# Six k loads of the first steps on ScalarE's queue, and the expert weights by half pairs, in an attention, mixture-of-experts and GELU kernel

## The chip, the cores and the metric

The kernel runs on one core of one Trainium2 chip. The metric is the device time of one execution in microseconds (us); lower is better.

## What is computed

Three layers follow each other. The first is a decayed linear attention (4 batches, 8 heads, 768 positions, 64 channels), the second a soft mixture of 8 experts with 4 slots each, the third a feed-forward layer with a sigmoid-GELU.

```python
for b in range(nb):                       # attention, block by block
    intra = einsum('bhic,bhjc->bhij', qb, kb) * Dmask
    intra = einsum('bhij,bhjd->bhid', intra, vb)
    inter = einsum('bhid,bhde->bhie', qb * lam_pow, kv_state)
    out[:, :, sl] = intra + inter
    kv_state = lam_block * kv_state + einsum('bhsd,bhse->bhde', kb * rev_pow, vb)
...
logits = x @ phi                          # x: 3072 x 512, phi: 512 x 32
slot_input = softmax(logits, 0).T @ x
h = maximum(slot_input[e] @ w1[e], 0.0)   # w1[e]: 512 x 1024
slot_out[e] = h @ w2[e]                   # w2[e]: 1024 x 512
x = softmax(logits, 1) @ slot_out
...
h = x @ w_in                              # w_in: 512 x 2048
return (h * (1.0 / (1.0 + exp(-1.702 * h)))) @ w_out
```

## The kernel before, in words

**Stages.** The attention comes first (to about 147 us of the profiled execution), then the experts (about 152 to 186 us), then the feed-forward layer, which is matmul after matmul to the end.

**Attention.** It has 32 steps (`NSTEP`), one for each pair of heads, half sequence (384 positions) and batch. The loop over `i` runs from -2 to 31 and is a hand-written pipeline under a manual schedule: in one round it does the scores of step i+1 (`do_SC`), the transposes of q and k of step i+2 (`do_T`, line 271 for q, 273 for k), the copy of q of step i+3 into another layout on ScalarE (`do_q`, line 262), the states (`do_ST`), the decayed k of step i+2 on ScalarE (`do_kd`, line 297) and the output of step i (`do_XS`, `do_XA`). Every fourth round does more, the tail of a finished group of four steps: logits, softmax pieces and slot sums.

**Loads.** `load_step` fetches q by one transfer (192 KB, line 126), and k and v by two transfers of 96 KB each, one per head (line 131). Their rooms are rings: three for q and three for k (pool `loads`), four for v. A load into a used room waits for the last reader of the step that had it. Before the change every one of these transfers is issued by SyncE (SP), whose queue takes them in the order of the program.

**Expert weights.** They are 32 pairs of 1 MB; `load_pair` issues one transfer per pair (line 170), or two of 512 KB for two of the pairs (line 168). Sixteen pairs have rooms of their own during the attention (`slots`), and `load_pairs(i)` decides how many of them are issued by round i. The other 16 wait for rooms that are freed at the attention's end (`slotb`, `slotc`) or by experts that are done. After them SP's queue has the first loads of the last layer's weights.

**Semaphores.** A transfer takes one of eight completion semaphores by turns, over both issuing engines together. An issue waits until the transfer that had its semaphore before has landed.

**Start.** ScalarE issues the load of `lam_b` (line 493), then loads its activation table and copies q of step 0. TensorE does eight warm-up matmuls meanwhile (line 501).

Of the kernel before, what the change touches and what calls it, by code (L numbers as in the profile page):

```python
# [17 lines left out]
def attention_moe_gelu_kernel(  # L18
# [14 lines left out]
    PE, ACT, DVE, POOL, SP = nc.tensor, nc.scalar, nc.vector, nc.gpsimd, nc.sync  # L33

    B, H, S, D = q.shape
    P = 128
    NHP = H // 2
    HS = 384
# [11 lines left out]
    NSTEP = NG * NHP  # L50
    NE = 1
    NPC = 16
# [58 lines left out]
    q_r, q_t, k_t, v_t = {}, {}, {}, {}  # L111

    def step_of(s):
        g, hp = divmod(s, NHP)
        b, hf = divmod(g, NHF)
        return b, hf, hp, g

    def load_step(s, what="qkv"):
        if s >= NSTEP:
            return  # L120
        b, hf, hp, g = step_of(s)
        t0 = hf * HS
        if "q" in what:

            q_r[s] = loads.tile([P, 2, R * D], F32, tag="qr", name="qr")
            SP.dma_start(out=q_r[s], in_=q[b, 2 * hp:2 * hp + 2, t0:t0 + HS, :].rearrange("h (p c) d -> p h (c d)", p=P))
        for src, nm, ts, bufs, pool in ((k, "k", k_t, 3, loads), (v, "v", v_t, 4, attn)):
            if nm in what:
                t = pool.tile([P, R, 2, D], F32, tag=nm, name=nm, bufs=bufs)
                for h in range(2):  # L130
                    SP.dma_start(out=t[:, :, h, :],  # L131
                                 in_=src[b, 2 * hp + h, t0:t0 + HS, :].rearrange("(c p) d -> p c d", p=P))
                ts[s] = t

# [4 lines left out]
    PC = 1024  # L139
    w_pc = {}  # L140
    worder = [("w1", 0)] + [we for e in range(1, E) for we in (("w1", e), ("w2", e - 1))] + [("w2", E - 1)]
    wlist = [(kind, e, j) for kind, e in worder for j in range(0, KD, 2)]
    nxt_w = [0]

    def pair_room(n):
        m = n % (NPC + NPC_B + NPC_C + NPC_D)
        if m == NPC + NPC_B + NPC_C:
            return [tailp.tile([P, PC], F32, tag="xn", name="w") for _ in range(2)]
        if m < NPC:
            return slots.tile([P, 2 * PC], F32, tag="w", name="w")  # L150
        return (slotb if m < NPC + NPC_B else slotc).tile([P, 2 * PC], F32, tag=f"w{m}", name="w", bufs=1)

    def load_pair(t=None):

        n = nxt_w[0]
        if n >= len(wlist):
            return
        nxt_w[0] += 1
        kind, e, j = wlist[n]
        if t is None:  # L160
            t = pair_room(n)
        src = w1[e, j * P:(j + 2) * P, :] if kind == "w1" else w2[e]
        src = src.rearrange("(p k) f -> p (k f)", p=P)
        o = 0 if kind == "w1" else j * PC
        parts = t if isinstance(t, list) else [t[:, :PC], t[:, PC:]]
        if isinstance(t, list) or n == len(wlist) - 1:
            for i in range(2):
                SP.dma_start(out=parts[i], in_=src[:, o + i * PC:o + (i + 1) * PC])
        else:
            SP.dma_start(out=t, in_=src[:, o:o + 2 * PC])  # L170
        w_pc[kind, e, j], w_pc[kind, e, j + 1] = parts
# [68 lines left out]
    def do_early(c):  # L240
        o = EARLY[c][-1]
        convert_abs(("early", c), o)
        by_turns(conversion(("early", c), o, POOL))
# [14 lines left out]
    def do_q(s):  # L258

        if s < NSTEP:  # L260
            q_t[s] = early.tile([P, R, 2, D], F32, tag="q", name="q", bufs=1)
            ACT.activation(out=q_t[s].rearrange("p c h d -> p h c d"),
                           in_=q_r[s].rearrange("p h (c d) -> p h c d", c=R), func=AF.Copy)
# [227 lines left out]
    with tc.manual_schedule():  # L491
# [7 lines left out]
        def warm_up(n):  # L499
            for _ in range(n):  # L500
                PE.matmul(bwarm, warm[:, :P], warm, start=True, stop=True)

        warm_up(8)
        for s, what in ((0, "qk"), (1, "qk"), (0, "v")):
            load_step(s, what)
        do_q(0)
        for h in range(2):
            r = slice(h * D, (h + 1) * D)
# [2 lines left out]
        def make_dec(h):  # L511

            DVE.tensor_tensor_scan(out=dec[:, h], data0=lam_b[:, h:h + 1].to_broadcast([P, P]), data1=ident,
                                   initial=0.0, op0=ALU.mult, op1=ALU.add)
# [4 lines left out]
        n = 1  # L519
        while n < P:  # L520
            DVE.tensor_tensor(out=qtab[:, :, n:2 * n], in0=qtab[:, :, 0:n],
                              in1=qtab[:, :, n - 1:n].to_broadcast([P, NHP, n]), op=ALU.mult)
            n *= 2
        load_step(1, "v")
        load_step(2, "k")
        load_step(2, "q")
        load_step(3, "q")
        for t in S_a + S_3:
            POOL.memset(t, 0.0)
# [2 lines left out]
        def make_isum():  # L532
            for j in range(G):
                for i in range(G):
                    POOL.tensor_copy(out=isum4[i * NS:(i + 1) * NS, j, :],
                                     in_=ident[i * NS:(i + 1) * NS, i * NS:(i + 1) * NS])

        def load_pairs(i):
            n = min(NPC, max(0, i + 1) * NPC // (NSTEP - 1), NPC - 1 if i < NSTEP - 5 else NPC)
            while nxt_w[0] < n:  # L540
                load_pair()

        for i in range(-2, NSTEP):
            g, ph = divmod(i, NHP)
            if i > -2:
                load_step(i + 5, "q")
            if i == 1:
                make_isum()

            if 0 <= i + 1 < NSTEP:  # L550
                do_SC(i + 1)
            if 0 < i + 2 < NHP:

                for h in range(2):
                    make_dec(2 * (i + 2) + h)

            if 0 <= i + 2 < NSTEP:
                do_T(i + 2)
                if i == -2:
                    warm_up(1)  # L560
            if i == NSTEP - 1:
                do_XS(i)
            if 0 <= i - 1 < NSTEP:
                do_XT(i - 1)
            if 0 <= i + 3 < NSTEP:
                do_q(i + 3)
            if ph == 1 and 0 <= g - 1 < NG:
                tail_L(g - 1)
            if ph == 2 and 0 <= g - 1 < NG:
                tail_max(g - 1)  # L570
            if ph == 3 and 0 <= g - 1 < NG:
                tail_exp(g - 1)
            if i == NSTEP - 1:
                tail_logits_first(NG - 1)
            if 0 <= i < NSTEP - 1:
                do_XS(i)

            if 0 <= i + 1 < NSTEP:
                do_ST(i + 1)
            if 0 <= i + 2 < NSTEP:  # L580
                do_kd(i + 2)
            if 0 <= i < NSTEP:
                do_XA(i)

            if ph == 0 and 0 <= g - 1 < NG:
                tail_logits(g - 1)
            if ph == 0 and 0 <= g - 2 < NG:
                tail_z(g - 2, "tk")
                tail_slot(g - 2)
                tail_acc(g - 2)  # L590
            if i == NSTEP - 4:
                load_pairs(i + 1)

            load_pairs(i)

            load_step(i + 5, "k")
            if i >= -1:
                load_step(i + 4, "v")
            c, turn = divmod(i - 2, EVERY)
            if turn == 1 and 0 <= c + 1 < len(EARLY):  # L600
                load_early(c + 1)
            if 0 <= i + 2 < NSTEP:
                do_qd(i + 2)
            if i == -2:
                load_step(2, "v")
                SP.dma_start(out=phi_sb, in_=phi.rearrange("(k p) s -> p k s", p=P))
            if turn == 0 and 0 <= c - 1 < len(EARLY):
                do_early(c - 1)
            if ph == 3 and 0 <= g - 1 < NG and i < NSTEP - 1:
                tail_row(g - 1)  # L610
            if ph == 0 and 0 <= g - 2 < NG:
                tail_row_exp(g - 2)
            if i == NSTEP - 3:
                while nxt_w[0] < NPC:
                    load_pair()
                loads_cm.__exit__(None, None, None)
                slotb_cm = tc.tile_pool(name="slotb", bufs=NPC_B, side="right", reuse_waits="tile")
                slotb = slotb_cm.__enter__()

                rooms = [pair_room(NPC + j) for j in range(NPC_B)]  # L620
                for t in rooms[::-1]:
                    load_pair(t)
            if i == NSTEP - 1:
                attn_cm.__exit__(None, None, None)
                early_cm.__exit__(None, None, None)
                slotc_cm = tc.tile_pool(name="slotc", bufs=NPC_C, side="left", reuse_waits="tile")
                slotc = slotc_cm.__enter__()
                rooms = [pair_room(NPC + NPC_B + j) for j in range(NPC_C)]
                for t in rooms:
                    load_pair(t)  # L630
# [219 lines left out]
        for f in range(2, NF):  # L850
            j = first_of[f] - 2 if f < HF else LATE_OUT.get(f, first_of[f] - 1)
# [68 lines left out]
        for kk in range(KD):  # L920
            src = bso[kk][:, None, :NS].to_broadcast([P, G, NS])
# [450 lines left out]
```

## Time and profile before

| | before |
|---|---|
| median of three runs | 476.57 us (475.67 to 476.94) |
| the profiled execution's own time | 477.57 us |
| its span, first to last instruction | 475.8 us |
| TensorE busy | 464.5 us, 98% of the span |
| DVE, ScalarE, GpSimd busy | 373.8, 302.7, 79.3 us |
| granted TensorE clock, mean | 0.999 of full speed |
| moved by DMA | 81.52 MB |

Busy time is what an engine spends in its own instructions; SP has none of those, its time is that of the transfers that it issues ("SPq", and "ACTq" for those that ScalarE issues). A transfer's landing is counted from its issue. "DMA share" is the mean busy share of the core's 16 DMA engines in a stretch.

### The profile page before, as it was taken

The numbers are of one execution on the slowest core, as the hardware profiler recorded it, in microseconds if no ns is written. First come the engines' busy times: TensorE is split into PE (matmuls) and PEld (weight loads), VectorE is DVE, ScalarE is ACT, GpSimd is POOL, SyncE is SP. The second block draws the span as 40 slices with busy tenths as digits, with TensorE's granted clock in tenths as the row PEclk, the third lists the DMA queues.
The fourth block names the chain that finished last, engine by engine and source line by source line (L and its number), as shares of the span: only waits on it lengthen the run. The fifth ranks groups of instructions, "written<-read, shape, count | busy, mean of one in ns | idle before, by whom it ended". The sixth has DMA issues, their size and how long they took to land.

```text
span 475.8 us, 10619 instructions
## 1 busy us (share of the span) xinstructions
PE 464.5 (98%) x3991; PEld 387.6 (81%) x3991; DVE 373.8 (79%) x901; ACT 302.7 (64%) x606; POOL 79.3 (17%) x129
## 2 busy tenths in 40 slices
PE   7999999999999998999999999999999999999996
PEld 4877877887876444787888778888899999999996
DVE  5866988988974344897787689998779989888985
ACT  5877678677754146866865867576665565565561
POOL 3624444444221010000000000000001111011104
PEclk9999999999999999999999999999999999999999
DMA  7899999999999997465643532100323331233034
GB/s 186 230 275 294 293 275 280 269 280 300 257 322 412 416 421 288 123 216 190 222 125 101 219 133 90 44 0 1 115 65 45 46 45 17 30 45 45 2 46 90
DMA packets 77476, 81.52 MB, mean 171 GB/s; under 512 B 54256, under 2 KB 62960, under 8 KB 73584
## 3 DMA queue, kind: packets, MB, share of 16 engines
q1 hardware_dynamic: 74832, 76.50, 51.2%
q0 software_dynamic: 2304, 4.20, 6.6%
q8 instruction: 32, 0.52, 0.5%
q14 instruction: 20, 0.16, 0.1%
q10 hardware_dynamic: 288, 0.14, 0.1%
HBM read 69.80 MB, written 11.01 MB: 170 GB/s over the span
## 4 chain that ended last, share of the span: by engine, by line
PE 80%; DMA 9%; DVE 6%; SPq 1%; issue 1%; ACT 1%; POOLq 0%; ACTq 0%; DVEq 0%
PE bo L1027 26%; PE bp L1195 25%; DMA w<-in_moe_w_dram 6%; PE bs L309 4%; PE bx L356 3%; PE bx L348 3%; PE bsh L1150 2%; PE bhh L980 2%; PE bq L271 2%; PE bst L322 2%; DMA qr<-in_q_dram 2%; PE bt L367 2%; PE bk L273 2%; DMA k<-in_k_dram 1%; SPq L131 1%; PE bp L449 1%
## 5 line engine op out<-in xcount | busy, mean ns | idle before, releaser
L1027 PE MATMUL bo<-wlo,GHI 128*128 128x512 f32 x192 | 75.3, 395 | 0.1
L1164 ACT ACTIVATE GHI<-G_all 128x896 fp32r<-128x896 f32 x48 | 45.8, 955 | 46.4 <-DVE G_all L1157 46.1
L1027 PE MATMUL bo<-whi,GLO 128*128 128x512 f32 x192 | 75.1, 394 | 0.0
L1027 PE MATMUL bo<-whi,GHI 128*128 128x512 f32 x192 | 74.8, 393 | 0.1
L1157 DVE TENSOR_TENSOR G_all<-G_all 128x128 f32<-128x128 f32 x192 | 47.3, 288 | 18.6 <-ACT G_all L1153 16.0
L1225 POOL DMA_DIRECT2D out_dram<-f x16 | 14.2, 1047 | 278.8 <-DVE G_all L1157 264.1
L1195 PE MATMUL bp<-tc,GHI 128*128 128x256 f32 x288 | 55.9, 282 | 0.0
L1169 DVE TENSOR_TENSOR GLO<-G_all,GHI 128x896 fp32r<-128x896 f32 x48 | 52.0, 1084 | 0.0
L988 ACT ACTIVATE G_all<-bhh 128x384 f32<-128x384 f32 x64 | 28.2, 489 | 34.5 <-PE bhh L980 34.4
L1195 PE MATMUL bp<-whi,GHI 128*128 128x256 f32 x192 | 49.5, 281 | 0.0
L1195 PE MATMUL bp<-wlo,GHI 128*128 128x256 f32 x192 | 49.2, 282 | 0.0
L1195 PE MATMUL bp<-whi,GLO 128*128 128x256 f32 x168 | 47.5, 283 | 0.0
L1195 PEld LDWEIGHTS bp<-tc,GHI 128*128 128x128 f32 x288 | 44.4, 190 | 0.0
L1027 PEld LDWEIGHTS bo<-wlo,GHI 128*128 128x128 f32 x192 | 36.0, 188 | 9.6 <-issue 2.5
L1027 PEld LDWEIGHTS bo<-whi,GLO 128*128 128x128 f32 x192 | 36.0, 188 | 7.8 <-DVE GLO L994 0.3
L1027 PEld LDWEIGHTS bo<-whi,GHI 128*128 128x128 f32 x192 | 36.1, 188 | 7.6 <-DVE W2s L934 0.5
L1195 PE MATMUL bp<-tc,GLO 128*128 128x256 f32 x144 | 40.4, 280 | 0.0
L290 POOL TENSOR_TENSOR qdT<-qT,qtab 128x384 f32<-128x384 f32 x32 | 32.4, 1014 | 40.7 <-PE bx L348 18.4
L994 DVE TENSOR_TENSOR GLO<-G_all,GHI 128x768 fp32r<-128x768 f32 x32 | 30.5, 954 | 10.5 <-ACT GHI L991 10.2
L1195 PEld LDWEIGHTS bp<-wlo,GHI 128*128 128x128 f32 x192 | 34.7, 189 | 0.0
L1195 PEld LDWEIGHTS bp<-whi,GHI 128*128 128x128 f32 x192 | 34.6, 189 | 0.0
L309 PEld LDWEIGHTS bs<-qT,kT 64*128 64x128 f32 x384 | 25.0, 187 | 11.8 <-DVE zsum L469 4.2
(234 smaller groups left out, 1036.7 us busy)
## 6 DMA issues: line engine op xcount, KB each, us to landing
w<-in_moe_w_dram SPq DMA_DIRECT2D x30, 1024.0 KB, 7.1
f<-in_moe_w_out_dram SPq DMA_DIRECT2D x15, 512.0 KB, 3.4
qr<-in_q_dram SPq DMA_DIRECT2D x32, 192.0 KB, 4.3
k<-in_k_dram SPq DMA_DIRECT2D x64, 96.0 KB, 5.5
v<-in_v_dram SPq DMA_DIRECT2D x64, 96.0 KB, 4.5
f<-in_moe_w_in_dram SPq DMA_DIRECT2D x12, 512.0 KB, 3.8
out_dram<-o SPq DMA_DIRECT2D x24, 256.0 KB, 2.6
out_dram<-f POOLq DMA_DIRECT2D x16, 256.0 KB, 4.8
```

The lines of the kernel that those rows point to most:

```text
L290: POOL.tensor_tensor(out=qdT[s], in0=qT[s].rearrange("m (c i) -> m c i", c=R), in1=qtab[:, hp, None, :].to_broadcast([P, R, P]), op=ALU.mult)
L309: PE.matmul(bs[h][:, cs], kT[s][hs, cs], qT[s][hs, cs], start=True, stop=True)
L348: PE.matmul(bx[:, c * P:(c + 1) * P], state(s, first + c), qdT[s][:, c, :], start=(c == chunks[0]), stop=False)
L356: PE.matmul(bx[h * D:(h + 1) * D, c * P:(c + 1) * P], v_t[s][:, c, h, :], AT[s, h][:, c, :], start=False, stop=(c == R - 1))
L988: ACT.activation(out=g[j][:, u * HS:(u + 1) * HS], in_=bh[j][u][:, :HS], func=AF.Gelu_apprx_sigmoid)
L994: DVE.tensor_tensor(out=glo[j][:, o], in0=g[j][:, o], in1=ghi[j][:, o].bitcast(F32), op=ALU.subtract)
L1027: PE.matmul(ob[t], a[j][:, t * P:(t + 1) * P], w[f], start=(begin and i == 0), stop=(end and i == 2))
L1157: DVE.tensor_tensor(out=o, in0=x, in1=y, op=op)
L1164: ACT.activation(out=sh[j], in_=gs(j)[:, P:], func=AF.Copy)
L1169: DVE.tensor_tensor(out=sl[j], in0=gs(j)[:, P:], in1=sh[j].bitcast(F32), op=ALU.subtract)
L1195: PE.matmul(bank_of(gi, i)[1], x, w, start=begin, stop=end)
L1225: POOL.dma_start(out=rows_of(gi, k), in_=cells[:, C11 + 2 * k:C11 + 2 * k + 2], accum_op=ALU.add)
```

## The change

Two things change. First, the k transfers of steps 0, 1 and 2 (six of them) are issued by ScalarE rather than by SP, ahead of ScalarE's first copy; q of step 2 moves ahead of v of step 1 on SP. Second, the 16 weight pairs that are loaded during the attention are each fetched by two transfers of 512 KB (`load_half`), and `load_pairs` counts halves: one per round from round -1 on, where before it was one whole pair about every second round from round 1 on.

```diff
-    def load_step(s, what="qkv"):
+    def load_step(s, what="qkv", eng=SP):
...
-            SP.dma_start(out=q_r[s], in_=q[b, 2 * hp:2 * hp + 2, t0:t0 + HS, :].rearrange("h (p c) d -> p h (c d)", p=P))
+            eng.dma_start(out=q_r[s], in_=q[b, 2 * hp:2 * hp + 2, t0:t0 + HS, :].rearrange("h (p c) d -> p h (c d)", p=P))
...
-                    SP.dma_start(out=t[:, :, h, :],
+                    eng.dma_start(out=t[:, :, h, :],
...
+    half_done = []
+
+    def load_half():
+
+        n = nxt_w[0]
+        kind, e, j = wlist[n]
+        src = w1[e, j * P:(j + 2) * P, :] if kind == "w1" else w2[e]
+        src = src.rearrange("(p k) f -> p (k f)", p=P)
+        o = 0 if kind == "w1" else j * PC
+        if not half_done:
+            half_done.append(pair_room(n))
+            SP.dma_start(out=half_done[0][:, :PC], in_=src[:, o:o + PC])
+            return
+        t = half_done.pop()
+        nxt_w[0] += 1
+        SP.dma_start(out=t[:, PC:], in_=src[:, o + PC:o + 2 * PC])
+        w_pc[kind, e, j], w_pc[kind, e, j + 1] = t[:, :PC], t[:, PC:]
...
-        for s, what in ((0, "qk"), (1, "qk"), (0, "v")):
-            load_step(s, what)
+        for s, what, eng in ((0, "q", SP), (0, "k", ACT), (1, "q", SP), (1, "k", ACT), (0, "v", SP), (2, "q", SP),
+                             (2, "k", ACT)):
+            load_step(s, what, eng)
...
         load_step(1, "v")
-        load_step(2, "k")
-        load_step(2, "q")
         load_step(3, "q")
...
-            n = min(NPC, max(0, i + 1) * NPC // (NSTEP - 1), NPC - 1 if i < NSTEP - 5 else NPC)
-            while nxt_w[0] < n:
-                load_pair()
+            n = min(2 * NPC, max(0, (i + 3) * 2 * NPC // (NSTEP + 1)), 2 * NPC - 2 if i < NSTEP - 5 else 2 * NPC)
+            while 2 * nxt_w[0] + len(half_done) < n:
+                load_half()
...
                 while nxt_w[0] < NPC:
-                    load_pair()
+                    load_half()
```

ScalarE's first instructions before, with the semaphores that they wait for (`lam_b` holds the decays, `qr` the loaded q, `bq` and `bk` the transposes of q and k):

```order
L493 DMA lam_b<-in_lam_dram 128x8
L262 ACT_TABLE_LOAD
L262 ACTIVATE q<-qr 128x2x3x64 [waits DMAHW1_49]
L281 ACTIVATE qT<-bq 128x3x128 [waits PE_49]
L284 ACTIVATE kT<-bk 128x384 [waits PE_49]
```

The same place of the changed kernel:

```order
L511 DMA lam_b<-in_lam_dram 128x8
L131 DMA k<-in_k_dram 128x3x64 x3
L131 DMA k<-in_k_dram 128x3x64 [waits DMAHW0_49]
L131 DMA k<-in_k_dram 128x3x64 [waits DMAHW2_49]
L131 DMA k<-in_k_dram 128x3x64 [waits DMAHW4_49]
L280 ACT_TABLE_LOAD
L280 ACTIVATE q<-qr 128x2x3x64 [waits DMAHW1_49]
```

Six issues now stand ahead of the table load, and the last three wait for semaphores: 0 is that of `lam_b`, 2 and 4 are those of the two k transfers of step 0.

SP's queue at the end of the attention before, from round 26 to the pairs whose rooms are freed (a `w` of 128x2048 is a whole pair, one of 128x1024 a half):

```order
L131 DMA k<-in_k_dram 128x3x64 x2
L131 DMA v<-in_v_dram 128x3x64 x2
L170 DMA w<-in_moe_w_dram 128x2048
L131 DMA v<-in_v_dram 128x3x64 x2
L170 DMA w<-in_moe_w_dram 128x2048 x7
```

The same place of the changed kernel:

```order
L131 DMA k<-in_k_dram 128x3x64 x2
L131 DMA v<-in_v_dram 128x3x64 x2
L164 DMA w<-in_moe_w_dram 128x1024
L131 DMA v<-in_v_dram 128x3x64 x2
L168 DMA w<-in_moe_w_dram 128x1024
L164 DMA w<-in_moe_w_dram 128x1024
L168 DMA w<-in_moe_w_dram 128x1024
L188 DMA w<-in_moe_w_dram 128x2048 x5
```

Behind the last v there were seven pairs; now there are three halves and five pairs, 512 KB less.

## Rows read from the trace of the kernel before

**Rows 1.** The page's first part: span, then TensorE's busy time, share and instructions.
```profile
span 475.8 us, 10619 instructions
...
PE 464.5 (98%) x3991; PEld 387.6 (81%) x3991; DVE 373.8 (79%) x901; ACT 302.7 (64%) x606; POOL 79.3 (17%) x129
```

**Rows 2.** Chain that ended last, 148 to 190 us: start, us, what.
```profile
154.88 12.23 DMA w<-in_moe_w_dram
...
167.12 17.53 DMA w<-in_moe_w_dram
...
184.70 1.05 PE bacc L789 x4
```

**Rows 3.** Timeline of PE, expert stage: start, us, instruction [idle before, releaser].
```profile
173.30 1.92 PE L789 MATMUL bacc<-w,hz 128*32 128x512 f32 x16
...
180.62 0.45 PE L736 MATMUL bc<-identr,cs 128*128 128x128 f32 x3
182.23 2.24 PE L789 MATMUL bacc<-w,hz 128*32 128x512 f32 x12 [1.16 <-DMA w<-in_moe_w_dram]
```

**Rows 4.** Busy time by stretch: length, engines, granted clock, DMA share, GB/s.
```profile
core 0: us, PE busy (x) PEld busy (x) DVE busy (x) ACT busy (x) POOL busy (x), PEclk, DMA share, GB/s
0.00:4.00 4.00, 3.23 (x8) 1.02 (x8) 0.10 (x1) 1.28 (x1) 1.91 (x15) 1.00 0.42 96
...
8.00:12.00 4.00, 3.08 (x44) 2.55 (x44) 3.81 (x13) 2.95 (x7) 1.34 (x3) 1.00 0.93 226
12.00:24.00 12.00, 12.00 (x173) 10.59 (x171) 9.60 (x31) 9.75 (x25) 7.67 (x20) 1.00 0.87 232
24.00:48.00 24.00, 22.53 (x285) 18.07 (x283) 16.71 (x48) 17.52 (x44) 8.73 (x11) 1.00 1.04 287
...
142.00:146.00 4.00, 3.98 (x43) 2.78 (x37) 1.39 (x6) 2.13 (x6) 0.35 (x1) 1.00 0.92 350
...
160.00:168.00 8.00, 8.00 (x116) 3.54 (x112) 2.67 (x6) 0.95 (x2) 0.94 (x3) 1.00 1.01 418
...
176.00:185.00 9.00, 7.17 (x68) 2.27 (x70) 3.29 (x11) 6.93 (x14) 0.00 (x0) 1.00 1.01 411
```

**Rows 5.** Timeline of the start, all engines.
```profile
0.73 0.45 ACTq L493 DMA_DIRECT2D lam_b<-in_lam_dram  x1
...
0.74 0.43 SPq L126 DMA_DIRECT2D qr<-in_q_dram  x1
...
1.21 1.28 ACT L262 ACT_TABLE_LOAD   x1 [1.21 <-PEq L1356]
1.23 0.99 SPq L131 DMA_DIRECT2D k<-in_k_dram  x2
...
3.90 0.34 DVE L509 COPY lamb<-lam_b 64x4 f32<-64x4 f32 x2 [3.90 <-DMA lam_b<-in_lam_dram]
4.13 0.52 ACT L262 ACTIVATE q<-qr 128x384 f32<-128x384 f32 x1 [1.64 <-DMA qr<-in_q_dram]
...
4.80 0.52 PE L271 MATMUL bq<-ident,q 128*128 128x128 f32 x3 [0.48 <-ACT q L262]
...
8.40 0.49 ACT L284 ACTIVATE kT<-bk 128x384 f32<-128x384 f32 x1
...
9.93 0.52 ACT L262 ACTIVATE q<-qr 128x384 f32<-128x384 f32 x1 [1.04 <-DMA qr<-in_q_dram]
```

**Rows 6.** DMA issues of 1.2 to 1.7 us: count, KB, us to landing.
```profile
k<-in_k_dram SPq DMA_DIRECT2D x1, 96.0 KB, 3.1
```

**Rows 7.** SP's waits, whole span: waiter, releaser, us in total, times, longest.
```profile
SPq L131 <- DMA w<-in_moe_w_dram: 3.6, 12, 0.7
```

**Rows 8.** Timeline of PE at the transposes of k, step 10.
```profile
43.20 0.52 PE L273 MATMUL bk<-ident,k 128*128 128x128 f32 x3 [1.05 <-DMA k<-in_k_dram]
```

**Rows 9.** Timeline of SP's queue at the attention's end.
```profile
131.21 0.48 SPq L170 DMA_DIRECT2D w<-in_moe_w_dram  x1
...
134.98 11.52 SPq L170 DMA_DIRECT2D w<-in_moe_w_dram  x7
```

## The prediction

> **What bounds the kernel now.** I read the page first: TensorE is busy 464.5 of 475.8 us [rows 1], so there are only 11.3 us in which it does nothing, and a change to transfers can give back no more than the part of these that waits for data. The chain that ended last shows where that is. In the expert stage it leaves TensorE: 12.23 and 17.53 us of it are landings of expert weights, the last at 184.66 us, and only then do the last four matmuls run [rows 2]. The stretches agree: at 160 to 168 us the DMA engines are fully busy at 418 GB/s [rows 4], and at 176 to 185 us TensorE is busy 7.17 of 9 us. So the experts end when the last weight lands, and everything later follows at TensorE's pace: a microsecond earlier or later there is a microsecond of the kernel.
>
> How much could be had there? Behind the last transposes at 180.62 + 0.45 us stand 16 matmuls, which without waits take about the 1.92 us of the 16 from 173.30 us on [rows 3]; they would end near 183.0 us, but end at 184.70 + 1.05 = 185.75 us [rows 2]. **Earlier weights are worth at most some 2.8 us**, as long as the attention doesn't end later.
>
> In the attention TensorE is the pace: 12.00 of 12 us at 12 to 24, 22.53 of 24 at 24 to 48 [rows 4]. The 1.47 us missing in the latter are nearly all one late k: 1.05 us at the transposes of step 10 [rows 8]. The DMA engines are at a share of about 1 from 24 us on, but are not full before: 0.93 at 8 to 12 us and 0.87 at 12 to 24, which leaves 4 x 0.07 + 12 x 0.13 = 1.84 us of them unused. At the start, step 2's q lets ScalarE wait 1.04 us [rows 5]: SP needs about 0.5 us for each issue (0.99 for two) and reaches that q late.
>
> **Edit 1: the weights by halves, sooner.** The order shows that behind the last v of the attention three halves and five pairs follow, where seven pairs did: 512 KB are ahead of that point. From there the engines are full until the last weight, so all that is gone from the backlog is gone from its end: 524,288 bytes at 418 GB/s [rows 4] are **1.25 us** earlier. It is a gain only if the DMA engines had room earlier (the 1.84 us say that they had) and if rooms don't hold the next pairs up. The pairs behind wait for rooms: SP's seven issues from 134.98 stretch over 11.52 us [rows 9], and at 142 to 146 us the rate falls to 350 GB/s [rows 4], (418 - 350) / 418 x 4 = 0.65 us below the full rate. If halves refill that dip the gain is 1.25 + 0.65 = 1.9 us; if the dip deepens by all that is saved, 0. I take 1.25, since the backlog behind the dip is long (the chain's landings last 12 to 18 us) and a pair's work is 2.5 us. The 16 added issues cost SP 16 x 0.48 us [rows 9] = 7.7 us over some 130 us; it has gaps between its issues, and they delay nothing as long as SP keeps ahead of the rooms.
>
> **Edit 2: k on ScalarE's queue.** It takes six issues, 3 us, out of SP's first ones, so q of step 2 comes early. But ScalarE is in order, and its table load and first copy stand behind the six. Worked out: `lam_b` is issued at 0.73 to 1.18 us [rows 5], three k by 1.18 + 3 x 0.5 = 2.7. The fourth waits for `lam_b` to land, which DVE's copy dates at 3.90: 3.9 to 4.4. The fifth waits for the first k, issued at 1.2 and landing 3.1 us later [rows 6], 4.3: 4.4 to 4.9. The sixth waits for the second, 1.7 + 3.1 = 4.8: 4.9 to 5.4. That an issue does wait for a landing is seen 12 times on SP, for weights [rows 7]. Then the table load, 1.28 us, to 6.7; before, it ended under the wait for q at 1.21 + 1.28 = 2.49. So **the first copy of q starts near 6.7 us where it started at 4.13**, 2.6 us later. Behind it are queued the transposes, the scores and everything of steps 0 and 1. By step 2 some is given back: from the first copy to the end of step 1's kT ScalarE needed 8.40 + 0.49 - 4.13 = 4.76 us, then waited for q [rows 5]. That wait goes, so step 2 starts at 6.7 + 4.76 = 11.5 instead of 9.93: **1.6 us late**. From below, landings that wait for nothing and issues of 0.43 [rows 5] give 1.3; from above, if the two queues' issues take turns and each of ScalarE's lasts 1.0, the three end at 4.2, the six at 7.2, the copy is at 8.5 and step 2 is 3.3 late.
>
> The Trainium skill has rules on this. DMA: Bandwidth & Descriptors, section Issuing engines are not separate DMA queues, says that a second engine saves only the issue time, usually small beside the transfer; here the row's 0.5 us per issue is not small beside the 0.23 us that 96 KB take at 418 GB/s. Perfetto Trace Analysis, section DMA Instruction - HWDGE, says that the descriptor generator is shared and locked by one issuer at a time; by that rule the upper price, 3.3 us, holds. The one overlap in this trace, 0.45 us on ScalarE beside 0.43 on SP from the same moment [rows 5], shows no such stretching.
>
> **What takes the lateness up.** At 12 to 24 us TensorE has no slack, so steps 2 to 5 stay 1.6 us late. At 24 to 48 us it has the 1.47. An attention that comes 1.6 us later finds its k landed, if k isn't later itself. It stands behind seven halves of weights by round 5 where before it was six: 1.25 us more work, against the 1.84 us of room before 24 us, of which I count 1.0 as used (SP itself waits longer, since step 3's k needs the room of step 0's, released by ScalarE's late copy of k). So k is about 0.3 us later, the attention 1.6, and the wait of 1.05 goes: 1.0 us is taken up (bounds 0 and 1.47), 0.6 stays. A later end of the attention shifts the freed rooms and so the last weights by as much.
>
> **Sum.** +1.6 - 1.0 - 1.25 = -0.65 us. The profiled execution, 477.57 us (1.8 outside its span), becomes 476.9; it lies 1.0 above the median of the runs, 476.57, which becomes **475.9 us**. What a measurement of this kernel tells from no change is about 0.3%, 1.4 us, so this counts as the same. Its own range: 1.3 to 1.9 late, 0.6 to 1.4 taken up, 1.25 gained: -1.35 to +0.05, 475.2 to 476.6.
>
> **Rivals.**
> - *The attention catches up wholly, and the halves fill the dip.* For it: the 1.47 us idle at 24 to 48 and the dip at 142 to 146 [rows 4]; a half holds up a k behind it half as long as a pair. Against: TensorE's full stretch before. The lateness is all but gone and the gain is 1.9: 474.7 us.
> - *Issues of the two queues take turns.* 3.3 late, 1.47 taken up, 1.25 gained: +0.6, 477.2 us. Against it is the overlap in rows 5; the skill's rule of the shared generator, above, is for it.
> - *The earlier halves push q and k back (the slower side).* Place: steps 8 to 11. By even rounds two halves more than before stand ahead of k (8 against 6 in round 6), 2.5 us of transfers, while the share is 1.04 already. If the room before 24 us isn't used, because SP stands behind ScalarE's late releases, step 11's k is 2.5 us and more late, and the attention with it: with 0.5 us of new idle time at the start 3.0 late, 1.25 gained: +1.8, 478.3 us. It decides from 1.25 + 1.4 = 2.7 us of lateness at step 11 on. For it: that k was late already. Against: TensorE waits for data almost nowhere later, so transfers have some slack.
> - *The granted clock falls.* TensorE's gap ahead of its first transposes grows from 0.48 to some 3 us. If the clock, 1.00 now in every stretch shown, is at its lower level (1.2 instead of 2.4 GHz) for the first steps, their matmuls (3.08 us busy at 8 to 12 us [rows 4], of which I put 2 on the chain) take 2 more: -0.65 + 2 = +1.35, 477.9 us.
>
> **Chances.** Forecast 0.45, catching up 0.27, taking turns 0.10, pushed back 0.14, clock 0.04. Of the forecast a tenth lies past -1.4. Faster by over 0.3%: 0.27 + 0.05 = 0.32; slower: 0.14 + half of the clock's and a little of the turns' = 0.18; within: 0.50. The range for 8 in 10 leaves out the far end of catching up and of the pushed back: 474.3 to 478.0.
>
> **What would show it.** ScalarE's issues of k until about 5.4 us, its table load after them, the first copy of q at 6.5 to 7.0; step 2's copy near 11.5; TensorE's bk wait of 1.05 us near 43 gone; DMA share over 0.9 at 12 to 24 us; the attention's end 0 to 1 us later; the last weight landing near 184.0 instead of 184.66 us. It is wrong if the first copy isn't late, if k waits of over 1 us stay or grow between 28 and 50 us, or if the last weight lands by more than 1.3 us earlier or any later.

## The result, and the profile after

The changed kernel took 482.08 us (median of six runs, 480.97 to 484.75), the kernel before 476.75 beside it (475.67 to 478.24). The ratio is 1.0128 [1.0106, 1.0149]: slower by more than 5 us, outside the range of the prediction and on the other side of its sign. The profiled execution took 482.14 us.

The first part of the page, as in [rows 1]:

```profile
span 480.4 us, 10637 instructions
...
PE 466.9 (97%) x3991; PEld 389.4 (81%) x3991; DVE 374.5 (78%) x901; ACT 303.2 (63%) x606; POOL 79.3 (17%) x129
```

The span grew by 4.6 us, TensorE's busy time by 2.4, so about half of the loss is new idle time and half is matmuls that last longer. The idle time and most of the longer matmuls are found at the start, the rest of these at 153 to 155 us (below). The timeline of all engines there, to be held against [rows 5]:

```profile
0.74 0.97 SPq L126 DMA_DIRECT2D qr<-in_q_dram  x2
...
1.20 5.82 ACTq L131 DMA_DIRECT2D k<-in_k_dram  x6
1.76 1.05 SPq L131 DMA_DIRECT2D v<-in_v_dram  x2
...
4.46 0.34 DVE L528 COPY lamb<-lam_b 64x4 f32<-64x4 f32 x2 [4.46 <-DMA lam_b<-in_lam_dram]
...
7.05 1.28 ACT L280 ACT_TABLE_LOAD   x1 [7.05 <-DMA k<-in_k_dram]
8.35 0.52 ACT L280 ACTIVATE q<-qr 128x384 f32<-128x384 f32 x1
...
9.02 0.87 PE L289 MATMUL bq<-ident,q 128*128 128x128 f32 x3 [4.67 <-ACT q L280]
...
11.11 1.63 PE L327 MATMUL bs<-qT,kT 64*128 64x128 f32 x12 [0.15 <-ACT kT L302]
...
12.18 0.90 SPq L131 DMA_DIRECT2D k<-in_k_dram  x2
...
14.17 0.52 ACT L280 ACTIVATE q<-qr 128x384 f32<-128x384 f32 x1
```

ScalarE's six issues stretch to 7.02 us, then comes the table load, and the first copy of q starts at 8.35 instead of 4.13. TensorE does nothing for 4.67 us, and its first matmuls then last longer: `bq` 0.87 us for 0.52, the scores `bs` 1.63 for 0.94 (before, at 6.41 us). SP is held up behind this: its k of step 3, issued at 12.18, needs the room of step 0's k, which ScalarE releases when it has made step 0's decayed k (`kd`, until 12.16); before, it went out at 8.14. Step 2's copy of q starts at 14.17 instead of 9.93, **4.24 us late where the prediction had 1.6**.

Two views say what stretched the issues. The timeline of ScalarE's queue shows the last three issues apart:

```profile
4.46 0.38 ACTq L131 DMA_DIRECT2D k<-in_k_dram  x1
...
5.72 0.37 ACTq L131 DMA_DIRECT2D k<-in_k_dram  x1
...
6.65 0.38 ACTq L131 DMA_DIRECT2D k<-in_k_dram  x1
```

And the DMA issues of 0.5 to 2.6 us, where the last number is the median time to landing in us; first the changed kernel, then the kernel before:

```profile
qr<-in_q_dram SPq DMA_DIRECT2D x2, 192.0 KB, 4.7
k<-in_k_dram ACTq DMA_DIRECT2D x3, 96.0 KB, 4.9
v<-in_v_dram SPq DMA_DIRECT2D x2, 96.0 KB, 5.5
lam_b<-in_lam_dram ACTq DMA_DIRECT2D x1, 4.0 KB, 3.7
```

```profile
qr<-in_q_dram SPq DMA_DIRECT2D x2, 192.0 KB, 3.4
...
lam_b<-in_lam_dram ACTq DMA_DIRECT2D x1, 4.0 KB, 3.1
```

An issue itself takes 0.4 to 0.5 us, as before. The landings take longer: q 4.7 us for 3.4, `lam_b` 3.7 for 3.1, k 4.9 for the 3.1 of [rows 6]. Each of the three waiting issues stands behind one of them.

Busy time by stretch, with the columns of [rows 4]:

```profile
8.00:12.00 4.00, 2.83 (x15) 2.17 (x17) 0.00 (x0) 2.94 (x7) 1.00 (x1) 1.00 0.61 129
12.00:24.00 12.00, 11.71 (x150) 9.89 (x150) 10.66 (x32) 8.78 (x22) 6.74 (x19) 1.00 0.84 210
24.00:48.00 24.00, 23.41 (x299) 20.14 (x300) 17.85 (x52) 18.62 (x46) 9.55 (x11) 1.00 1.06 295
...
153.00:155.00 2.00, 2.00 (x24) 1.00 (x21) 0.93 (x3) 1.53 (x3) 0.00 (x0) 0.50 0.99 418
```

Between 8 and 24 us the DMA engines moved 129 x 4 + 210 x 12 = 3036 KB, before 226 x 4 + 232 x 12 = 3688 KB: the room that earlier weights were to fill was not filled, it grew. At 24 to 48 us TensorE idles 0.59 us instead of 1.47, all of it in one wait for k, here of step 9:

```profile
42.95 0.52 PE L291 MATMUL bk<-ident,k 128*128 128x128 f32 x3 [0.59 <-DMA k<-in_k_dram]
```

The wait at step 10 of [rows 8] is gone, and so is one of 0.42 us at step 8. The lateness of the scores against before is 4.7 to 4.9 us in steps 2 to 7, 4.26 in step 8, 5.04 in step 9 and 3.80 in step 10 (51.07 against 47.27 us). So about 1.1 us is taken up there, near the 1.0 that was predicted, out of a larger lateness. TensorE at the attention's end:

```profile
150.49 0.53 PE L385 MATMUL bt<-ident,xT 128*128 128x128 f32 x3
...
153.49 1.91 PE L663 MATMUL bp<-xn,e 128*32 128x256 f32 x12
...
156.88 1.50 PE L787 MATMUL bh<-w,sT 128*32 128x256 f32 x23
```

The last transposes of the attention start 3.54 us late (146.95 before). The experts start 4.86 late (152.02 before), because in this execution the granted clock fell to 0.50 at 153 to 155 us (the windows above) and the twelve `bp` took 1.91 us for 1.04. The chain that ended last, as in [rows 2]:

```profile
159.74 11.54 DMA w<-in_moe_w_dram
...
171.29 17.75 DMA w<-in_moe_w_dram
...
189.09 1.05 PE bacc L806 x4
```

It still leaves TensorE for the landings of weights, and the last matmuls of the experts start 4.39 us later than at 184.70. The weights came late with the attention, and no microsecond of the 1.25 shows.

### The profile page after: what moved, and what is told of

Its sections match the earlier page's. It is cut to its first block, busy times and chain, and to the rows that moved or that the text cites. A ratio compares the mean times of both kernels' runs of the same rounds, so it can differ in the third digit from the quotient of the medians.

```text
span 480.4 us, 10637 instructions
## 1 busy us (share of the span) xinstructions
PE 466.9 (97%) x3991; PEld 389.4 (81%) x3991; DVE 374.5 (78%) x901; ACT 303.2 (63%) x606; POOL 79.3 (17%) x129
## 4 chain that ended last, share of the span: by engine, by line
PE 82%; DMA 12%; DVE 2%; ACT 1%; issue 1%; SPq 1%; ACTq 0%; POOLq 0%; DVEq 0%
PE bo L1044 26%; PE bp L1212 25%; DMA w<-in_moe_w_dram 8%; PE bs L327 5%; PE bx L374 3%; DMA k<-in_k_dram 3%; PE bx L366 3%; PE bq L289 2%; PE bsh L1167 2%; PE bst L340 2%; PE bhh L997 2%; PE bt L385 2%; PE bk L291 2%; PE bl L395 1%; PE bp L467 1%; PE bp L663 1%
## 5 line engine op out<-in xcount | busy, mean ns | idle before, releaser
L1242 POOL DMA_DIRECT2D out_dram<-f x16 | 14.2, 1047 | 278.3 <-DVE G_all L1174 249.0
L330 DVE TENSOR_TENSOR AT<-bs,dec 128x384 f32<-128x384 f32 x64 | 32.5, 550 | 6.7 <-PE bs L327 6.0
L299 ACT ACTIVATE qT<-bq 128x384 f32<-128x384 f32 x32 | 22.6, 705 | 20.6 <-PE bq L289 19.5
```

The source lines that it names most:

```text
L299: ACT.activation(out=t.rearrange("m (p c) -> m c p", c=R), in_=bq[:, :HS].rearrange("m (c p) -> m c p", c=R), func=AF.Copy)
L330: DVE.tensor_tensor(out=t, in0=bs[h][:, :HS].rearrange("m (c i) -> m c i", c=R), in1=dec[:, 2 * hp + h, None, :].to_broadcast([P, R, P]), ...
```

## The experiments

Twelve runs followed (e1 and e5 are the same kernel). "Last `bt`" is the start of the attention's last transposes and "experts" the end of the experts' last matmuls, both against the profile of before. These two come from one execution each; executions of the kernel before lay between 474.85 and 479.83 us, so a microsecond in them decides nothing, while the ratios come from several runs.

| run | median us | ratio to before | first copy | step 2's copy | last `bt` | experts |
|---|---|---|---|---|---|---|
| before | 476.75 | 1 | 4.13 | 9.93 | 0 | 0 |
| changed | 482.08 | 1.0128 [1.0106, 1.0149] | 8.35 | 14.17 | +3.54 | +4.39 |
| e1 halves only | 477.58 | 1.0018 [0.9998, 1.0038] | | | | |
| e5 the same again | 477.69 | 1.0028 [1.0004, 1.0052] | 4.32 | 10.21 | -0.05 | +0.22 |
| e2 k on ScalarE only | 480.67 | 1.0090 [1.0070, 1.0111] | 8.56 | 14.66 | +3.34 | +3.10 |
| e3 only step 0's k there | 477.64 | 1.0025 [1.0006, 1.0043] | 4.86 | 11.24 | +1.04 | +0.91 |
| e4 28 warm-up matmuls | 482.87 | 1.0131 [1.0101, 1.0160] | 8.46 | 13.10 | +3.42 | +2.95 |
| e6 order on SP only | 476.82 | 1.0008 [0.9988, 1.0028] | 4.33 | 10.46 | -1.42 | -1.65 |
| e7 table load earlier | 481.20 | 1.0098 [1.0072, 1.0125] | 7.74 | 14.05 | +2.68 | +2.50 |
| e8 one pair later | 477.18 | 1.0013 [0.9997, 1.0028] | 4.22 | 10.34 | -2.21 | -0.88 |
| e10 k on GpSimd | 479.87 | 1.0071 [1.0043, 1.0099] | 4.28 | 12.15 | +0.80 | +1.80 |
| e11 first copy on VectorE | 480.89 | 1.0089 [1.0058, 1.0120] | 4.94 | 13.08 | +3.26 | +3.39 |
| e12 q on ScalarE, no waits | 478.33 | 1.0031 [1.0011, 1.0050] | 5.21 | 11.03 | +0.27 | +0.01 |
| e13 order, 12 warm-ups | 477.42 | 1.0017 [0.9999, 1.0035] | 4.13 | 10.06 | +0.09 | -0.07 |

### One edit at a time: e1 and e2

e1 keeps the halves and puts all k back on SP, in the old order:

```diff
-        for s, what, eng in ((0, "q", SP), (0, "k", ACT), (1, "q", SP), (1, "k", ACT), (0, "v", SP), (2, "q", SP),
-                             (2, "k", ACT)):
-            load_step(s, what, eng)
+        for s, what in ((0, "qk"), (1, "qk"), (0, "v")):
+            load_step(s, what)
...
         load_step(1, "v")
+        load_step(2, "k")
+        load_step(2, "q")
```

> Only the weights by halves, one round apart and two rounds sooner; all k on SP as before. Theory A (the loss is ScalarE's late start, passed on whole): first copy of q at 4.1 us, and the time is that of the kernel before or up to 1.25 us less (475.3 to 476.8); the last weight lands 0 to 1.25 us earlier than 184.66. Theory B (the halves are the loss: more issues, more waits for a semaphore, k and q pushed back): 2 us slower or more, 478.7 and up, with waits for k and q at TensorE and ScalarE of over 2 us more between 20 and 60 us.

e2 keeps the k on ScalarE and has whole pairs at the rounds of before:

```diff
-            n = min(2 * NPC, max(0, (i + 3) * 2 * NPC // (NSTEP + 1)), 2 * NPC - 2 if i < NSTEP - 5 else 2 * NPC)
-            while 2 * nxt_w[0] + len(half_done) < n:
-                load_half()
+            n = min(NPC, max(0, i + 1) * NPC // (NSTEP - 1), NPC - 1 if i < NSTEP - 5 else NPC)
+            while nxt_w[0] < n:
+                load_pair()
```

> Only the six k issues on ScalarE; weights by whole pairs as before. Theory A: first copy of q near 8.3 us, step 2 some 4.2 us late, of which about 1 us is taken up by the late k of step 10; the time is 3.5 to 5.5 us over before (480.3 to 482.3). Theory B: the delay at the start is mostly taken up because SP's queue has room; at most 2 us slower (478.7).

Measured: the halves alone +0.18% (between the two theories), the k alone +0.90% (inside theory A), both together +1.28%. The k are 0.0090 x 476.77 = 4.3 us of the loss. e2's ScalarE shows the same picture as the changed kernel:

```profile
1.20 6.03 ACTq L131 DMA_DIRECT2D k<-in_k_dram  x6
7.27 1.28 ACT L280 ACT_TABLE_LOAD   x1 [7.27 <-DMA k<-in_k_dram]
8.56 0.52 ACT L280 ACTIVATE q<-qr 128x384 f32<-128x384 f32 x1
```

So the late start comes without the halves, and the halves alone don't gain. One of e1's twelve executions, the profiled one, lasted 1148.73 us against 476 to 480 of the others; it is in the median of the table (477.34 without it) but not in the ratio. The rows of this kernel come from e5.

### Where the half went: e5 and e8

e5 is e1 again.

> The kernel with the halves alone once more, for its profile. Theory F (the freed rooms are the gate, so that the dip at the attention's end takes what the half saves): the attention ends 0 to 0.5 us later than before, the rate between 141 and 147 us is 40 to 100 GB/s below that of before, and the last weight lands within 0.5 us of 184.66. Theory G (the half did come off the end, but k and q came later): the attention ends 1 us or more later, with more waits for k and q between 28 and 50 us, and the last weight lands as much later less 1.25 us. Time 476.5 to 478.5 by both.

Measured: 1.0028 [1.0004, 1.0052]. The attention ends as before (-0.05 us), and the experts 0.22 later. The stretch of 139 to 141 us of e5:

```profile
139.00:141.00 2.00, 2.00 (x27) 1.71 (x22) 1.72 (x6) 1.23 (x4) 0.38 (x1) 1.00 0.75 197
```

and of the kernel before:

```profile
139.00:141.00 2.00, 2.00 (x26) 1.71 (x23) 1.71 (x6) 1.23 (x4) 0.43 (x1) 1.00 1.00 422
```

SP's queue of e5 has the last halves out by 133.45 us and the next pair at 139.50:

```profile
132.78 0.67 SPq L168 DMA_DIRECT2D w<-in_moe_w_dram  x1
139.50 7.09 SPq L188 DMA_DIRECT2D w<-in_moe_w_dram  x5
```

In the kernel before the pair that fills this room was issued at the same time:

```profile
139.56 0.33 SPq L170 DMA_DIRECT2D w<-in_moe_w_dram  x1
```

The room, not the queue, sets that moment. In e5 the engines run dry before it: at 139 to 141 us they move (422 - 197) x 2 = 450 KB less, nearly the whole half. In this pair of profiles the dip takes what the edit saves. It comes sooner than theory F has it: over 141 to 147 us the rate is only some 30 GB/s lower.

That the half alone deepened the dip is not shown, because whole pairs do it too. SP waits for that room first on transposes of k, then 2.6 us on ScalarE's `kd`. The first of these waits (us in total, times, longest; 128 to 148 us) in the kernel before, in e5 and in e6 (whole pairs, below):

```profile
SPq L170 <- PE bk L273: 1.0, 1, 1.0
```

```profile
SPq L188 <- PE bk L291: 3.5, 1, 3.5
```

```profile
SPq L170 <- PE bk L273: 4.8, 1, 4.8
```

So SP stood before the room for 3.6 us before, 6.1 in e5 and 7.4 in e6. e2, with whole pairs, also waits 4.7 us there, and its rate falls to 156 GB/s at 143 to 145 us. In the profile of before SP came to the room late, since the last loads of v kept it until 134.98 us; in e6 it was through with them at 129.41. e6's rate falls before that, to 262 and 238 GB/s at 137 to 141 us. The room is the gate in all four.

e8 goes the other way: before, with one pair (1 MB) more left for behind the last v.

```diff
-            n = min(NPC, max(0, i + 1) * NPC // (NSTEP - 1), NPC - 1 if i < NSTEP - 5 else NPC)
+            n = min(NPC, max(0, i + 1) * NPC // (NSTEP - 1), NPC - 1 if i < NSTEP - 5 else NPC) - 1
```

> The kernel before with one weight pair less issued at every round of the attention, so that 1 MB more stands behind the last v. Price by the backlog alone: 1,048,576 bytes at 418 GB/s, 2.5 us later. Less what the dip has room for (0.65 to 0.85 us) and what earlier k and q give back at steps 8 to 11 (up to 1.4 us): 0.2 to 1.9 us slower, 477 to 478.7. If the weights' end is no pace at all: 475.5 to 476.7.

Measured: +0.13% [-0.03, +0.28], at the near end of the expected range, where 1 MB more behind a full queue would be 2.5 us or 0.5%. In its profile the attention ended 2.21 us earlier and the experts only 0.88; from one execution that is no more than a hint that the megabyte cost 1.3 us and the attention gained it, since e6's attention also ended 1.42 us earlier with no weight moved. So the time doesn't follow the backlog in this direction either: between half a megabyte less and a megabyte more it moves by at most some tenths of a per cent. Why the halves cost 0.2 to 0.3% instead of nothing stays open.

### What makes the start late: e3, e7 and e12

e3 leaves only step 0's k on ScalarE (whole pairs, order of before):

```diff
-        for s, what in ((0, "qk"), (1, "qk"), (0, "v")):
-            load_step(s, what)
+        for s, what, eng in ((0, "q", SP), (0, "k", ACT), (1, "q", SP), (1, "k", SP), (0, "v", SP)):
+            load_step(s, what, eng)
```

> Only the two k transfers of step 0 on ScalarE, which wait for no semaphore; k of steps 1 and 2 on SP, whole pairs. Theory A (the waits for landings and the queueing behind them make the late start): issues to 2.2 us, table load to 3.5, first copy within 0.3 us of 4.13; time 475.5 to 477.2. Theory C (two queues at once slow each transfer's landing, so that q of step 0 lands late whatever ScalarE waits for): q of step 0 lands 4.4 us or more after its issue where it was 3.4, first copy at 5.0 us or later, and the kernel is 0.5 to 1.5 us slower than before.

Measured: +0.25% [+0.06, +0.43], between the two theories. Nothing on ScalarE waits for a semaphore now, and its table load starts at 2.31 us. The first copy waits for the landing:

```profile
4.86 0.52 ACT L280 ACTIVATE q<-qr 128x384 f32<-128x384 f32 x1 [1.27 <-DMA qr<-in_q_dram]
```

It is still late (4.13 to 4.33 us with all on SP: before, e5, e6, e8, e13): q takes 4.2 us to land, and k 4.7 on either queue. Two transfers on ScalarE's queue are enough to stretch the landings of both. Whether the second queue does it, or that more is issued sooner (six transfers of q and k by 2.7 us, four before), isn't separated.

e12 moves three transfers of q to ScalarE instead, placed so that the turns of the eight semaphores leave it without a wait:

```diff
+        for s, what, eng in ((0, "q", ACT), (0, "k", SP), (1, "q", ACT), (1, "k", SP), (2, "q", ACT), (0, "v", SP),
+                             (2, "k", SP)):
+            load_step(s, what, eng)
```

> The kernel before with q of steps 0, 1 and 2 (three transfers of 192 KB) issued by ScalarE and all k by SP; the semaphores' turns then leave ScalarE's issues without any wait. Whole weight pairs as before. Theory A (the waits of ScalarE's fourth to sixth issue made the lateness): three issues by 2.7 us, table load to 4.0, first copy when q lands, 4.6 to 5.9 us, 0.5 to 1.8 late; 477.0 to 478.5 us (+0.1 to +0.4%). Rival C (two queues at once, and the low clock after them, cost most of it): first copy 6 us or later, step 2 at 12.5 or later, 479 us or more.

Measured: +0.31% [+0.11, +0.50], inside what theory A gives and 2.3 us below e2's median, though as many bytes (3 x 192 KB) go through ScalarE. Its ScalarE:

```profile
1.20 1.50 ACTq L126 DMA_DIRECT2D qr<-in_q_dram  x3
2.73 1.28 ACT L280 ACT_TABLE_LOAD   x1 [2.73 <-issue]
5.21 0.52 ACT L280 ACTIVATE q<-qr 128x384 f32<-128x384 f32 x1 [1.20 <-DMA qr<-in_q_dram]
```

In the changed kernel ScalarE's six issues lasted 5.82 us, of which the three gaps ahead of the fourth to sixth are 3.2 (1.7, 0.9 and 0.6 us). e12 drops these and three issues as well, so by the rows the waits are the larger part of the loss, and a second queue without waits is still no gain.

e7 puts the table load into the wait ahead of ScalarE's fourth k, by a tiny activation there:

```diff
+                    if eng is ACT and s == 1 and h == 0:
+                        ACT.activation(out=sgl, in_=nc.const_aps.tensor(1.0, (P, 1), F32), func=AF.Copy)
```

> The changed kernel with the table load moved between ScalarE's third and fourth k, where it stands under the wait for a landing (one tiny copy of a constant is added for it). Theory A (each us at the start is a us at the end): first copy at 7.1 to 7.5 us where it was 8.35, 0.9 to 1.3 us come back: 480.8 to 481.2. Theory H (the transfers take over as the pace by step 10, as the kernel with the longer warm-up suggests, which was 1.07 us earlier at step 2 and not at all at step 9): nothing comes back, 481.5 to 483.

Measured: 481.20 us, 0.9 below the changed kernel, the intervals overlap. The table load indeed goes to 2.76 us, but the fourth issue moved as well:

```profile
2.76 1.28 ACT L134 ACT_TABLE_LOAD   x1 [2.76 <-issue]
...
6.23 1.46 ACTq L131 DMA_DIRECT2D k<-in_k_dram  x3
7.74 0.52 ACT L282 ACTIVATE q<-qr 128x384 f32<-128x384 f32 x1 [3.48 <-DMA v<-in_v_dram]
```

It now goes out at 6.23 us where it went at 4.46, so of the 1.28 us only 0.61 comes back at the first copy. The turns have changed: SP's third q now goes out when `lam_b` lands (4.52), and ScalarE's fourth k at the moment when step 1's q lands (issued at 1.22, 5.0 us to landing). The landing of v in the row is what the profile puts ahead of the copy at 7.74, behind the sixth issue. e7 doesn't separate theory A from no gain; it shows that which landing an issue waits for is a matter of the turns.

### Who has to wait: e10 and e11

e10 issues the six k from GpSimd instead of ScalarE (`POOL` for `ACT` in the list of loads).

> The changed kernel, halves and all, with the six k issued by GpSimd instead of ScalarE. Theory A (ScalarE is in order, and its first copy stands behind issues that wait for landings): ScalarE is free again, its table load starts near 1.2 us and its first copy when q of step 0 lands, 4.1 to 5.4 us. k is now issued behind GpSimd's mask work (1.9 us) and lands later, so the first transposes of k may wait 1 to 3 us; time 477.5 to 480. Rival C (what costs is that a second queue feeds the engines at once, whichever engine issues): q of step 0 lands at 5.4 us or later as in the changed kernel, step 2 starts near 14, and the time stays at 481 to 482.5.

Measured: 479.87 us, the slow end of what theory A gives. Of its start:

```profile
1.50 4.82 POOL L131 DMA_DIRECT2D k<-in_k_dram  x6 [0.19 <-issue]
...
4.28 0.52 ACT L280 ACTIVATE q<-qr 128x384 f32<-128x384 f32 x1 [1.80 <-DMA qr<-in_q_dram]
...
7.16 0.87 PE L291 MATMUL bk<-ident,k 128*128 128x128 f32 x3 [1.33 <-DMA k<-in_k_dram]
```

The first copy is on time again (q lands in 3.7 us here), so it was ScalarE's queue that held it. But GpSimd takes 0.8 us for each issue and k is late, and step 2 starts 2.2 us late. Of the runs that keep the halves and change the start (e4, e7, e10, e11) it is the only one whose interval lies clear below that of the changed kernel.

e11 keeps the six issues on ScalarE and moves step 0's copy of q to VectorE:

```diff
+            if s == 0:
+                DVE.tensor_copy(out=q_t[s].rearrange("p c h d -> p h c d"),
+                                in_=q_r[s].rearrange("p h (c d) -> p h c d", c=R))
+                return
```

> The changed kernel with the first copy of q (step 0) on VectorE; ScalarE keeps its six issues, and its table load. Theory A: the copy starts when q lands, near 5.4 us, TensorE's first transposes near 6.1 instead of 9.02; but ScalarE still can't copy their results before its table load ends at 8.3, where it copied q until 8.87 and then waited for the transposes; so about 1.5 to 2 us of the 4.2 of lateness go: 480 to 480.7 us. Rival (the late clock and the stretched landings alone set step 2): under 0.5 us go, 481.6 to 482.5.

Measured: 480.89 us, 1.2 below the changed kernel, with overlapping intervals. The copy starts at 4.94 us, and TensorE then waits for ScalarE's copies of the transposes, which still stand behind the table load:

```profile
7.18 1.28 ACT L303 ACT_TABLE_LOAD   x1 [7.18 <-DMA k<-in_k_dram]
...
9.53 1.65 PE L331 MATMUL bs<-qT,kT 64*128 64x128 f32 x12 [1.90 <-ACT kT L306]
```

The first scores are 1.6 us earlier than in the changed kernel, as expected, but by the third step (17.55 against 17.61 us) nothing of it is left: TensorE ran at the low clock there (0.50 at 12 to 14 us).

### The clock, and the order alone: e4, e6 and e13

e4 is the changed kernel with `warm_up(28)` for `warm_up(8)`, which fills TensorE's gap until 8.96 us.

> The changed kernel with 28 warm-up matmuls where it has 8, so that TensorE is busy through the gap of 4.67 us ahead of its first transposes. Theory A says that the gap lets the clock fall: the transposes of step 0 take 0.52 us again (0.87 in the changed kernel) and the scores 0.94 (1.63), and 0.7 to 1.3 us come back: 480.8 to 481.4. If the lower rate there lies under other waits, nothing comes back: 482.1.

Measured: 482.87 us, no difference from the changed kernel. TensorE's rows of e4:

```profile
9.13 0.52 PE L289 MATMUL bq<-ident,q 128*128 128x128 f32 x3 [0.17 <-ACT q L280]
...
29.66 0.52 PE L291 MATMUL bk<-ident,k 128*128 128x128 f32 x3 [0.78 <-DMA k<-in_k_dram]
...
42.92 0.52 PE L291 MATMUL bk<-ident,k 128*128 128x128 f32 x3 [0.72 <-DMA k<-in_k_dram]
```

The matmuls have their full rate, and step 2's copy starts at 13.10 instead of 14.17: the low clock was 1.07 us of the lateness there. Waits for k give it back: after the first of 0.78 us, which the changed kernel doesn't have, 0.10 is left (scores of step 6 at 32.92 us for 33.02), and the scores of step 9 start at 45.74 us, 45.77 in the changed kernel. So behind the clock stood late transfers, ready to take its place. The granted clock didn't fall at 153 us in this profile, so that fall isn't what makes the changed kernel 5 us slower.

e6 is the kernel before with q and k of step 2 ahead of v of step 1, all on SP; e13 has the same order, and `warm_up(12)`.

> All on SP, whole pairs; only the order of its first issues changes: q and k of step 2 ahead of v of step 1. The copy of step 2's q then waits no longer: it starts at 8.9 to 9.1 where it started at 9.93, 0.8 to 1.0 us earlier. If TensorE is the pace behind it, 0.8 to 1.0 us come off the end (475.8 to 476.0); if the transfers are the pace at steps 8 to 11, the waits there grow by as much and the time stays (476.5 to 477).

> The kernel before with q and k of step 2 ahead of v of step 1, all on SP, whole pairs, and 12 warm-up matmuls instead of 8 (they end near 4.5 instead of 4.3 us). If the low clock of 5 to 9 us that the profile of the order alone showed (first transposes 0.87 us) hid a gain of about 1 us of that order: first transposes 0.52 us, step 2's copy near 9.4, 475.3 to 476.2 us. If the start isn't what sets the end by then, or the clock was a matter of that one execution: 476.5 to 477.2, no difference.

Measured: 1.0008 [0.9988, 1.0028] and 1.0017 [0.9999, 1.0035], no difference. In e13 the twelve matmuls lasted 5.28 us rather than the expected 3.7, so that TensorE was still busy when the copy of q was done, and its first transposes start 1.05 us later than before:

```profile
5.85 0.75 PE L271 MATMUL bq<-ident,q 128*128 128x128 f32 x3
```

The wait of 1.04 us for step 2's q, which started the thought of two queues, is gone in both, but step 2 starts no earlier (10.46 and 10.06 us for 9.93): e6's first matmuls ran slowly (`bq` 0.87 us), e13's warm-up ran long. So the order alone gains nothing measurable, and what an earlier step 2 would be worth isn't shown. None of the twelve beats the kernel before.

## Why the prediction was wrong

- **"So the first copy of q starts near 6.7 us where it started at 4.13": the step that failed.** The mechanism held: six issues, three of which wait for landings, then the table load, then the copy (e10 takes them off ScalarE and the copy is back at 4.28). Its sizes came from landings of a single queue. With two queues `lam_b` landed 0.56 us later, and the two k of step 0, behind which the fifth and sixth issue stand, in 4.5 to 4.9 instead of 3.1 us: sixth issue at 6.65 for 4.9, and copy at 8.35 for 6.7. The landings were the term that was mis-sized, by 1.65 us.
- **"Step 2 starts at 11.5 instead of 9.93: 1.6 us late".** It started at 14.17. From the first copy to step 2's ScalarE took 14.17 - 8.35 = 5.82 us, not 4.76; the 1.06 more are the low clock, since e4, at the full rate, took 13.10 - 8.46 = 4.64. The rival of the clock had a chance of 0.04 for a gap that the prediction itself put at 3 us, and was priced at 2; at the end e4 gives nothing of it back. 11.5 + 1.65 + 1.06 = 14.2 us accounts for the place.
- **The upper bound of that step had nearly the right number for another reason.** Its case "if the two queues' issues take turns" gave a copy at 8.5. The issues did not take turns: three on ScalarE from 1.20 to 2.73 us and four on SP from 0.74 to 2.81 took 0.5 us each, side by side. The Trainium skill (Perfetto Trace Analysis, section DMA Instruction - HWDGE) has the issuers lock a shared generator; no row here shows an issue lengthened by it. The Trainium skill (DMA: Bandwidth & Descriptors, section Issuing engines are not separate DMA queues) says that transfers of all issuers interleave on the same 16 engines. The trace is in line with that: with more transfers under way, 3.1 us to landing became 4.9. The Trainium skill says there too that a second engine saves only issue time; here even that saving, three issues of SP without a wait (e12) or six with waits (e2), was worth nothing.
- **"1.0 us is taken up".** 1.1 us was, between steps 7 and 10: the waits of 0.42 at step 8 and 1.05 at step 10 went, as was said of the latter, and one of 0.59 us at step 9 came. The step was right in size, with a wait that it didn't foresee.
- **"I take 1.25" for the weights: the second step that failed.** The prediction had named the value that came, "if the dip deepens by all that is saved, 0", and set it aside because the backlog behind the dip is long. In e5 the dip was deeper by 450 of 512 KB: the freed room sets when the next pair goes out (139.50 us, before 139.56). A dip as deep in e6 and e2 shows that SP stands before that room with whole pairs too, so the part of the halves in it is open. The measured effect of the halves is +0.2 to +0.3%, on the other side of 0, and why it isn't 0 stays open.
- **The rival "earlier halves push q and k back"** was on the right side. Its condition came true, SP behind ScalarE's late releases (652 KB less moved from 8 to 24 us), but not its price: with the k on ScalarE the halves end the attention only 0.20 us later than whole pairs do (+3.54 against e2's +3.34), and without (e5) not at all.
- **Sum with the sizes found:** +0.90% from the k (e2) and +0.18 to +0.28% from the halves (e1, e5) make 1.08 to 1.18% or 5.1 to 5.6 us; both together measured 1.28% [1.06, 1.49] or 6.1 us, and 5.3 by the medians. The parts account for the whole within intervals of about 1 us each.

## What to carry to other kernels

A load on a compute engine's queue costs more than its issue: if the issue waits for a semaphore, everything that the engine computes waits for somebody's landing, and landings measured with one queue need not hold for two. Count the waits that an order of semaphores puts ahead of the first useful instruction, and move only transfers that have none. Where the next transfer waits for a room, less work ahead of it lets the queue run dry earlier and need not bring the end forward.

## What the runs showed of the hardware

- Landings of the same first transfers grew with ScalarE as a second issuer, in the changed kernel (q 4.7, k 4.9, `lam_b` 3.7 us) and with only two transfers there (e3: 4.2, 4.7, 3.9), against 3.4, 3.1 and 3.1 before; with all on SP, e5, e6, e8 and e13 have 3.3 to 3.7, 3.1 to 3.4 and 2.9 to 3.2. With GpSimd as the second issuer, whose issues are 0.8 us apart, q took 3.6 (e10). So it may be the number of transfers under way, and not the second queue, that stretches them.
- The level of TensorE's clock is better read from durations than from its column. At 8 to 12 us of the changed kernel the column says 1.00, while the scores lasted 1.63 us; in e11 and e12 they lasted 1.65 and 1.66 with 0.56 and 0.50 in the column, near the lower of the two levels (1.2 GHz). Over the profiles, the first scores ran at the full rate after a gap of TensorE of up to 0.54 us ahead of the first transposes (before, e4, e8, e13) and in e5 after 0.63, but slowly after 0.60 (e10), 0.65 (e6) and all longer ones. Gaps that near to each other at either level give no limit.
